# The second norm's turned rows in DRAM: one row of 512 behind the other in the order of the partitions, instead of 32 groups of 8

## The chip, the cores and the metric

The kernel runs on one core of a Trainium2 chip. The time is the device time of one execution in microseconds (us): before the change the median of three runs is 1620.35 us (1619.17 to 1622.79). The core has five engines that run side by side, each with its own instruction stream in order: TensorE (PE) for matmuls, VectorE (DVE), ScalarE (ACT), GpSimd (POOL) and SyncE (SP), which issues nearly all DMAs here. A DMA moves data between DRAM and the core's own memory (SBUF) on up to 16 DMA engines. Matmul results land in banks of a second small memory, PSUM, each of 128 partitions x 512 fp32.

## The reference

One transformer block with adaptive layer norm, in fp32: x has 2048 rows of D = 512.

```python
mod = (_silu(c) @ w_mod).reshape(c.shape[0], 6, 1, -1)
sa, ca, ga, sb, cb, gb = (mod[:, 0], ..., mod[:, 5])
h = _layernorm(x) * (1 + ca) + sa
x = x + ga * _A_ref(h, A_wq, A_wk, A_wv, A_wo)     # 32 heads of 16, one shared key and value head
h = _layernorm(x) * (1 + cb) + sb                  # the second norm
x = x + gb * _B_ref(h, B_w1, B_w2)                 # relu(h @ w1) @ w2, Dff = 1792
return x
```

`_A_ref` is attention of all 2048 rows over all 2048 keys, softmax(q k / 4) v for each head, then a product with wo. The change concerns how h of the second norm gets from the row layout, where the norm is computed, into the turned layout, where `h @ w1` needs it.

## The kernel before, in words

Attention is walked in 32 units: 8 blocks of TB = 256 query rows times NG = 4 groups of heads. For each unit and each of the 16 key tiles (KT) of 128 keys, `scores` (L856) makes four score tiles of 128x512 in PSUM, ACT takes their exponentials into `pe` (L858), and `values` (L999) multiplies these with the values: on PE one step for one key tile, 512 steps in all. One unit ahead, `max_of` (L514, reduced by DVE at L516) computes the maxima that the exponentials subtract.

Between these steps PE does other work in portions (L162 to L178, and L153 to L158 at start and end): for block b the output projection, the first dense layer and the second one. All of this "behind" work of block b runs in the 64 steps of the next block's attention; `behind(b)` (L599) yields it portion by portion. Steps of the other engines that belong to it are put at places in the stream by `at(slot, ...)` (L625): a slot is one step of a key tile, and slot n of block b comes at about step (b + 1) * 64 + n, counted from 0. The order of all instructions is written out by hand, so an engine that reaches an instruction whose data isn't there holds up what is queued behind it.

The second norm of block b (seven blocks; the eighth goes another way in `behind_last` at the end, through PE) takes these steps:

- slots 12 to 20: statistics of the two tiles of 128 rows on DVE, the normed rows `xn` (128 partitions = rows, 512 columns) on POOL, with scale and shift;
- slots 21 and 23, `turn_of(t)` (L647): DVE turns blocks of 32x32 inside `xn` into `xt` (L649), and SyncE writes `xt` to a DRAM tile `xdr` (L651). After the 32x32 turn, partition 32 i + a of `xt` holds, for column number a of every 32-column block, the rows 32 i to 32 i + 31;
- slot 24, `load_turned` (L659): four reads (L663) fetch `xh` from `xdr`, each into 32 partitions, so that a partition holds four columns of h (one of every 128) and along each the 256 rows. They wait for both writes;
- slot 27: two calls of `split` (L255): ACT rounds `xh` to the high part `hh` (L256), and POOL subtracts to get the low part `hl` (L257), since products in the fast fp32 form are made of such parts;
- `dense1` (L575) then multiplies `hh` and `hl` with the first layer's weights; its matmuls show at L175.

In SyncE's queue the order around it is: first write of `xdr`, two loads of the next queries (`qp<-qdr`, L445), second write, the four reads, then the maxima of the next unit (`mdr<-ms`, L478, and `qp<-mdr`, L484). `xdr` has two buffers, so a block writes into another one than the block before; `xh` takes the buffer of `xn`. In block 0 the portions of other work in front of the dense layer are empty (`fill`, L613), so PE has less to do per step there.

Of the kernel before, what the change touches and what calls it, by code (L numbers as in the profile page):

```python
# [9 lines left out]
F32 = mybir.dt.float32  # L10
# [8 lines left out]
S, D, H, DH, DFF = 2048, 512, 32, 16, 1792  # L19
P = 128  # L20
# [4 lines left out]
TT = TB // P  # L25
# [37 lines left out]
def build(tc, nc, cst, sb, ps, dr, x, wq, wk, wv, wo, w1, w2, c, w_mod, out):  # L63
# [11 lines left out]
    def ps_fill():  # L75
        return ps.tile([P, 512], F32, name="ps_fill", tag="fill", bufs=1)
# [149 lines left out]
    def ln_mv(n):  # L226
        return sb.tile([P, n, 2], F32, name="mv", tag="mv", bufs=4)
# [8 lines left out]
    def rsqrt(ve, n, late):  # L236
        y = sb.tile([P, n], F32, name="y", tag="y", bufs=2)
        u = sb.tile([P, n], F32, name="u", tag="u", bufs=2)
        yi = y.bitcast(I32)
        nc.vector.tensor_scalar(yi, ve.bitcast(I32), 1, None, op0=OP.logical_shift_right)  # L240
        nc.vector.tensor_scalar(yi, yi, -1.0, float(0x5f3759df), op0=OP.mult, op1=OP.add)
        for _ in range(3):
            if late:
                nc.vector.tensor_tensor(u, y, y, op=OP.mult)
                nc.vector.scalar_tensor_tensor(u, u, -0.5, ve, op0=OP.mult, op1=OP.mult)
                nc.vector.scalar_tensor_tensor(y, u, 1.5, y, op0=OP.add, op1=OP.mult)
            else:
                nc.gpsimd.tensor_tensor(u, y, y, op=OP.mult)
                nc.gpsimd.tensor_tensor(u, u, ve, op=OP.mult)
                nc.gpsimd.tensor_scalar(u, u, -0.5, 1.5, op0=OP.mult, op1=OP.add)  # L250
                nc.gpsimd.tensor_tensor(y, y, u, op=OP.mult)
        return y
# [25 lines left out]
    def add_psum(dst, pt, other):  # L278
        stg = stage()[:, 0:pt.shape[-1]]
        nc.scalar.activation(stg, pt, AF.Copy)  # L280
        nc.gpsimd.tensor_tensor(dst, stg, other, op=OP.add)
# [267 lines left out]
    def flat(t, k2):  # L549
        return t[:, k2 * 2:k2 * 2 + 2].rearrange("p a n -> p (a n)")  # L550

    def open_block(b):
        x1 = sb.tile([P, TT, D], F32, name="x1", tag="x1", bufs=2)
        nc.sync.dma_start(x1, chunks(x[b * TB:(b + 1) * TB]))
        x1s[b] = x1
        return x1, [sb.tile([P, DC, TB], F32R, name=n, tag="t4", bufs=2) for n in ("oh", "ol")]
# [11 lines left out]
    def normed(x1, xn, ts, nm, y, eng):  # L568
        for n, t in enumerate(ts):
            eng.tensor_scalar(xn[:, t], x1[:, t], nm[:, n:n + 1], y[:, n:n + 1],  # L570
                              op0=OP.add, op1=OP.mult)
            eng.tensor_tensor(xn[:, t], xn[:, t], cbr, op=OP.mult)
            eng.tensor_tensor(xn[:, t], xn[:, t], sbr, op=OP.add)
# [6 lines left out]
    def dense2(b, t, pt):  # L580
        ts = slice(t * P, (t + 1) * P)
        todo = []
        for f in range(FC):
            i, fi = divmod(f, 8)
            rh, rl = r4s[b][i * 2], r4s[b][i * 2 + 1]
            w = w2r[f // 2]
            for n, (a, p) in enumerate(((rh, 0), (rh, 1), (rl, 0))):
                todo.append(("f32r", pt, a[:, fi, ts], w[:, p, f % 2],
                             f + n == 0, f == FC - 1 and n == 2))
        return todo  # L590
# [8 lines left out]
    def behind(b):  # L599
        def in_parts(todo, n):  # L600
            for i in range(0, len(todo), n):
                yield todo[i:i + n]

        def second(b, t):
            pt = ps_fill()
            yield from in_parts(dense2(b, t, pt), 6)
            ot = sb.tile([P, D], F32, name="ot", tag="tmp", bufs=2)
            add_psum(ot, pt, x1s[b][:, t])
            nc.sync.dma_start(out[b * TB + t * P:b * TB + (t + 1) * P], ot)

        x1, oo = open_block(b)
        if b == 0:
            rest, fill = iter([[]] * 3), [[]] * 7  # L613
        else:
            rest, fill = carried.pop(), second(b - 1, 1)
        yield next(rest)
        yield next(rest)
        for k2 in range(DC // 2):
            put_off.append(partial(split, flat(oo[0], k2), flat(oo[1], k2), flat(on[b], k2)))
        yield from rest  # L620
        xn = sb.tile([P, TT, D], F32, name="xn", tag="xn", bufs=1)
        xdr = dr.tile([32, TT, 4, D], F32, name="xdr", tag="xdr", bufs=2)
        mvs = [ln_mv(1) for t in range(TT)]

        def at(slot, *steps):  # L625
            slots.setdefault((b + 1) * 64 + slot, []).extend(steps)

        def norm_of(t, *where):
            st = sb.tile([P, 2, nc.vector.BN_STATS_DIM], F32, name="st2", tag="st2", bufs=2)
            mv = mvs[t]  # L630
            ve = sb.tile([P, 1], F32, name="ve", tag="ve", bufs=2)
            nm = sb.tile([P, 1], F32, name="nm", tag="nm", bufs=2)

            def ends():
                nc.vector.bn_aggr(mv[:, 0], st)
                nc.vector.tensor_scalar(ve, mv[:, :, 1], EPS, None, op0=OP.add)
                nc.gpsimd.tensor_scalar(nm, mv[:, :, 0], -1.0, None, op0=OP.mult)

            def rows():
                normed(x1, xn, (t,), nm, rsqrt(ve, 1, False), nc.gpsimd)  # L640

            for n in range(2):
                at(where[n], partial(nc.vector.bn_stats, st[:, n], x1[:, t, n * TB:(n + 1) * TB]))
            at(where[2], ends)
            at(where[3], rows)

        def turn_of(t):  # L647
            xt = sb.tile([P, D], F32, name="xt", tag="tmp", bufs=2)
            nc.vector.transpose(xt.rearrange("p (j k n) -> p k j n", j=4, k=DC),  # L649
                                xn[:, t].rearrange("p (k j n) -> p k j n", j=4, k=DC))  # L650
            nc.sync.dma_start(xdr[:, t].rearrange("a i n -> i a n"), xt)  # L651

        hp = []
        norm_of(0, *(12, 13, 14, 16))
        norm_of(1, *(17, 18, 19, 20))
        at(21, partial(turn_of, 0))
        at(23, partial(turn_of, 1))

        def load_turned():  # L659
            xh = sb.tile([P, TT * 4, DC, 32], F32, name="xh", tag="xn", bufs=1)  # L660
            pieces = xdr.rearrange("a t i (j m) -> j a (t i) m", j=4)
            for j in range(4):
                nc.sync.dma_start(xh[j * 32:(j + 1) * 32].rearrange("p q k n -> p q (k n)"),  # L663
                                  pieces[j])
            for k2 in range(DC // 2):
                ks = slice(k2 * 2, k2 * 2 + 2)
                at(27, partial(split, *[h[:, ks].rearrange("p k (q n) -> p k q n", n=32)
                                        for h in hp],
                               xh.rearrange("p q k n -> p k q n")[:, ks]))

        at(24, load_turned)
        for t in range(TT):
            pt = ps_fill()
            yield from in_parts(out_proj(pt, oo, t), 6)
            if t == 0:
                add_psum(x1[:, t], pt, x1[:, t])
            else:
                add_psum(x1[:, t, 0:TB], pt[:, 0:TB], x1[:, t, 0:TB])
                nc.vector.tensor_tensor(x1[:, t, TB:], pt[:, TB:], x1[:, t, TB:], op=OP.add)
        ahead = [load_w1(f) for f in range(2)]  # L680

        hp += [sb.tile([P, DC, TB], F32R, name=n, tag="t4", bufs=2) for n in ("hh", "hl")]
        yield from fill
        r4 = r4s[b] = [sb.tile([P, 8, TB], F32R, name="r4", tag="big", bufs=4) for _ in range(4)]
        for f2 in range(FC // 2):
            pt = ps_fill()
            for f in range(f2 * 2, f2 * 2 + 2):
                if f + 2 < FC:
                    ahead.append(load_w1(f + 2))
                yield dense1(pt[:, (f % 2) * TB:(f % 2 + 1) * TB], ahead.pop(0), hp)  # L690
            i, f = divmod(f2 * 2, 8)
            put_off.append(split_psum(
                r4[i * 2][:, f:f + 2].rearrange("p a n -> p (a n)"),
                r4[i * 2 + 1][:, f:f + 2].rearrange("p a n -> p (a n)"), pt, AF.Relu))
        first_half = second(b, 0)
        yield from itertools.islice(first_half, 4)
        carried.append(first_half)
# [225 lines left out]
    for j in range(8):  # L923
# [14 lines left out]
                 t=itertools.chain(*trs), k=itertools.chain(*kvs),  # L938
# [3 lines left out]
    for what in FIRST:  # L942
# [23 lines left out]
        elif what == "s":  # L966
            n = next(sums3)
# [39 lines left out]
    for c in range(NU * KT // 2):  # L1007
# [7 lines left out]
        else:  # L1015
            if not portion:
                banks.extend([ps_max, ps_max, ps_max, ps_fill] * 2)
            u, i, j = places.pop(0)
# [83 lines left out]
```

## Time and profile before

One execution was profiled. Its own time is 1621.31 us, its span (first to last instruction) 1619.5 us.

| what | before |
| --- | --- |
| median of three runs | 1620.35 us (1619.17 to 1622.79) |
| profiled execution | 1621.31 us |
| its span | 1619.5 us |
| PE / DVE / ACT / POOL busy | 1601.0 / 1351.0 / 1210.8 / 383.9 us |
| mean granted clock of PE | 0.999 |
| DMA moved | 137.16 MB in 96198 packets |
| `xdr<-xt` | 14 DMAs of 256 KB, issued from 338.8 to 1445.4 us |
| `xh<-xdr` | 28 DMAs of 128 KB, issued from 350.6 to 1453.8 us |

How to read it: in the profile, `L651` is line 651 of the kernel, `xdr<-xt` names what is written and what is read, `x14` is a count. PE's busy time is the union of matmuls that overlap, and their ends are modelled, so a share near 99% doesn't mean that nothing is late: lateness shows as longer steps between the groups of L999. "Idle before" is the time an engine stood still ahead of an instruction, with the one that ended it. The chain that ended last is followed back from the last instruction to whatever released each step. PEclk is the granted share of PE's clock. In the view by stretches, each row has the stretch, its length, the busy time of PE, PEld (weight loads), DVE, ACT and POOL with the count of instructions, then the granted clock, the mean busy share of the 16 DMA engines, and GB/s. Where the text says a step, it is the time from the start of one group of eight L999 instructions to the next.

### The profile page before, as it was taken

The numbers are of one execution on the slowest core, as the hardware profiler recorded it, in microseconds if no ns is written. First come the engines' busy times: TensorE is split into PE (matmuls) and PEld (weight loads), VectorE is DVE, ScalarE is ACT, GpSimd is POOL, SyncE is SP. The second block draws the span as 40 slices with busy tenths as digits, with TensorE's granted clock in tenths as the row PEclk, the third lists the DMA queues.
The fourth block names the chain that finished last, engine by engine and source line by source line (L and its number), as shares of the span: only waits on it lengthen the run. The fifth ranks groups of instructions, "written<-read, shape, count | busy, mean of one in ns | idle before, by whom it ended". The sixth has DMA issues, their size and how long they took to land.

```text
span 1619.5 us, 33365 instructions
## 1 busy us (share of the span) xinstructions
PE 1601.0 (99%) x12817; PEld 896.0 (55%) x12817; DVE 1351.0 (83%) x2366; ACT 1210.8 (75%) x2372; POOL 383.9 (24%) x584
## 2 busy tenths in 40 slices
PE   9999999999999999999999999999999999999999
PEld 6555554436655565546655565546645565546468
DVE  6888889998889888998889888998889888898031
ACT  4467778778877787778877787778877788778831
POOL 4323455531113110141112211131112211131110
PEclk9999999999999999999999999999999999999999
DMA  8335543213211331214201331113201331113331
GB/s 281 105 114 155 177 115 97 87 55 108 70 36 40 96 105 30 61 43 126 70 22 48 98 105 32 56 48 115 82 20 50 88 105 41 46 59 105 118 121 59
DMA packets 96198, 137.16 MB, mean 85 GB/s; under 512 B 24040, under 2 KB 59564, under 8 KB 96040
## 3 DMA queue, kind: packets, MB, share of 16 engines
q1 hardware_dynamic: 95768, 134.83, 27.6%
q8 instruction: 102, 1.67, 0.4%
q14 instruction: 56, 0.46, 0.1%
q10 hardware_dynamic: 272, 0.20, 0.0%
HBM read 104.00 MB, written 28.82 MB: 82 GB/s over the span
## 4 chain that ended last, share of the span: by engine, by line
PE 91%; DMA 3%; DVE 3%; ACT 1%; issue 1%; SPq 0%; POOL 0%; POOLq 0%; ACTq 0%; DVEq 0%
PE ps_pv L999 30%; PE ps_exp L856 21%; PE ps_fill L175 17%; PE ps_max L514 16%; DVE pm L516 2%; PE ps_fill L158 2%; PE ps_exp L158 1%; DMA xdr<-xt 1%; PE ps_max L158 1%; DMA qdr<-qq 1%; ACT pe L858 1%; PE ps_exp L358 1%; PE ps_exp L149 1%; DMA xh<-xdr 1%; SPq L663 0%
## 5 line engine op out<-in xcount | busy, mean ns | idle before, releaser
L516 DVE TENSOR_REDUCE pm<-ps_max 128x1 f32<-128x512 f32 x2002 | 1247.5, 682 | 152.6 <-PE ps_max L514 108.3
L858 ACT ACTIVATE pe<-ps_exp 128x512 f32<-128x512 f32 x2010 | 1061.9, 604 | 294.4 <-PE ps_fill L175 125.2
L514 PE MATMUL ps_max<-kp,qp 48*128 48x512 f32 x2002 | 822.9, 423 | 1.4 <-DMA qp<-qdr 0.9
L856 PE MATMUL ps_exp<-qp,kp 50*128 50x512 f32 x2010 | 750.2, 415 | 6.9 <-ACT pe L858 6.5
L999 PE MATMUL ps_pv<-pe,vt 128*32 128x512 f32 x4096 | 546.9, 605 | 0.0
L856 PEld LDWEIGHTS ps_exp<-qp,kp 50*128 50x128 f32 x2010 | 352.2, 185 | 296.1 <-ACT pe L858 190.6
L514 PEld LDWEIGHTS ps_max<-kp,qp 48*128 48x128 f32 x2002 | 364.4, 185 | 239.6 <-DVE pm L516 206.3
L175 PE MATMUL ps_fill<-w2r,r 64*128 64x512 f32 x1008 | 274.7, 404 | 0.0
L175 PE MATMUL ps_fill<-hh,w1s 64*128 64x256 f32 x1456 | 211.4, 285 | 0.0
L175 PEld LDWEIGHTS ps_fill<-hh,w1s 64*128 64x128 f32 x1456 | 191.1, 186 | 0.1
L175 PEld LDWEIGHTS ps_fill<-w2r,r 64*128 64x128 f32 x1008 | 174.7, 185 | 7.3
L999 PEld LDWEIGHTS ps_pv<-pe,vt 128*32 128x32 f32 x4096 | 81.3, 108 | 127.5 <-issue 108.4
L257 POOL TENSOR_TENSOR r<-stg,r 128x512 fp32r<-128x512 f32 x49 | 62.8, 1283 | 293.1 <-ACT r L256 286.1
L175 PE MATMUL ps_fill<-hl,w1s 64*128 64x256 f32 x728 | 117.1, 281 | 0.0
L175 PEld LDWEIGHTS ps_fill<-hl,w1s 64*128 64x128 f32 x728 | 97.4, 185 | 0.0
L175 PE MATMUL ps_fill<-hT,wq 64*128 64x256 f32 x320 | 90.6, 399 | 0.0
L1062 POOL TENSOR_TENSOR on<-num,den 128x256 f32<-128x256 f32 x31 | 22.8, 737 | 221.6 <-DMA den<-recs 142.7
L175 PEld LDWEIGHTS ps_fill<-hT,wq 64*128 64x128 f32 x320 | 54.0, 185 | 2.3
L873 POOL COPY num<-pvs 128x256 f32<-128x256 f32 x32 | 12.8, 399 | 162.7 <-ACT pvs L869 151.8
L475 POOL TENSOR_TENSOR ms<-sq,ms 128x32 fp32r<-128x32 f32 x28 | 7.2, 256 | 141.2 <-ACT ms L470 141.2
L268 ACT ACTIVATE stg<-ps_fill 128x512 f32<-128x512 f32 x64 | 39.4, 615 | 0.3 <-PE ps_fill L158 0.2
L175 PE MATMUL ps_fill<-wol,oh 64*128 64x512 f32 x112 | 36.8, 408 | 0.0
(177 smaller groups left out, 1025.0 us busy)
## 6 DMA issues: line engine op xcount, KB each, us to landing
w1s<-w1dr SPq DMA_DIRECT2D x104, 512.0 KB
qp<-qdr SPq DMA_DIRECT2D x64, 192.0 KB
qdr<-qq SPq DMA_DIRECT2D x45, 256.0 KB
raw<-in_B_w_dram SPq DMA_DIRECT2D x28, 256.0 KB
w1dr<-w1s SPq DMA_DIRECT2D x14, 512.0 KB
wmod<-in_w_mod_dram SPq DMA_DIRECT2D x6, 1024.0 KB
x<-in_A_x_dram SPq DMA_DIRECT2D x8, 512.0 KB
out_dram<-ot SPq DMA_DIRECT2D x16, 256.0 KB
```

The source lines that it names most:

```text
L149: nc.tensor.matmul(pt[:, 0:P], idn, idn, start=True, stop=True)
L158: nc.tensor.matmul(pt, w, a, start=start, stop=stop)
L175: ins = nc.tensor.matmul(pt, w[r], a[r], start=start and h == 1, stop=stop and h == 0)
L257: (eng or nc.gpsimd).tensor_tensor(lo, src, hi.bitcast(F32), op=OP.subtract)
L268: nc.scalar.activation(stg, pt, func, **kw)
L358: nc.tensor.matmul(pt, wkv[:, k * P:(k + 1) * P], hT[b][:, k], start=k == 0, stop=k == DC - 1)
L514: nc.tensor.matmul(pt, qps[u][i][r, j * P:(j + 1) * P], kp[r, kb * 512:(kb + 1) * 512], start=True, stop=True)
L516: nc.vector.tensor_reduce(pms[u][:, (hf * 2 + i) * 4 + j, kb:kb + 1], pt, axis=AX.X, op=OP.max)
L856: nc.tensor.matmul(pt, kp[r, kt * P:(kt + 1) * P], qps[u][ct // 2][r], start=True, stop=True)
L858: nc.scalar.activation(pe, pt, AF.Exp)
L999: nc.tensor.matmul(pvt[at:at + 32], vt[:, kt], pes.pop((s, i)), start=(kt == 0), stop=(kt == KT - 1))
L1062: due[1]()
```

## The change

The DRAM tile `xdr` between the write and the reads gets another order of dimensions. Before, it was [32, TT, 4, 512]: for each a of 32, for each tile t, for each i of 4, a row of 512 numbers. Partition p = 32 i + a of `xt` went to row (a, t, i). After, it is [TT, 128, 512]: for each tile t the 128 partitions in their order. The sizes, the number of DMAs and who issues them stay; the pattern by which the write walks DRAM, and that of the reads, change.

```diff
-        xdr = dr.tile([32, TT, 4, D], F32, name="xdr", tag="xdr", bufs=2)
+        xdr = dr.tile([TT, P, D], F32, name="xdr", tag="xdr", bufs=2)
...
-            nc.sync.dma_start(xdr[:, t].rearrange("a i n -> i a n"), xt)
+            nc.sync.dma_start(xdr[t], xt)
...
-            pieces = xdr.rearrange("a t i (j m) -> j a (t i) m", j=4)
+            pieces = xdr.rearrange("t (i a) (j m) -> j a (t i) m", a=32, j=4)
```

On the SBUF side nothing changes: `xt` is written from 128 partitions of 512 numbers each, and each of the four reads fills 32 partitions of `xh` with eight pieces (t, i) of 128 numbers. In DRAM the eight pieces of a partition lay 2 KB apart and the partitions 16 KB apart; now the eight pieces lie 64 KB apart and the partitions 2 KB apart.

## The prediction

> **What bounds the kernel.** I read the page first, for the engine with the least idle time and the chain that ended last.
>
> ```profile
> span 1619.5 us, 33365 instructions
> PE 1601.0 (99%) x12817; PEld 896.0 (55%) x12817; DVE 1351.0 (83%) x2366; ACT 1210.8 (75%) x2372; POOL 383.9 (24%) x584
> PE 91%; DMA 3%; DVE 3%; ACT 1%; issue 1%; SPq 0%; POOL 0%; POOLq 0%; ACTq 0%; DVEq 0%
> PE ps_pv L999 30%; PE ps_exp L856 21%; PE ps_fill L175 17%; PE ps_max L514 16%; DVE pm L516 2%; PE ps_fill L158 2%; PE ps_exp L158 1%; DMA xdr<-xt 1%; PE ps_max L158 1%; DMA qdr<-qq 1%; ACT pe L858 1%; PE ps_exp L358 1%; PE ps_exp L149 1%; DMA xh<-xdr 1%; SPq L663 0%
> ```
>
> TensorE carries 91% of the chain, so only what makes TensorE late can move the end. Yet the two transfers that the change touches, `xdr<-xt` and `xh<-xdr`, stand on that chain. The views of who waited for whom (SyncE's queue, ACT, PE; columns: total us, times, longest) say how much they hold up.
>
> ```profile
> SPq L663 <- DMA xdr<-xt: 41.3, 7, 6.0
> ACT hh L256 <- DMA xh<-xdr: 3.7, 6, 1.8
> ACT hh L256 <- issue: 0.4, 1, 0.4
> PE ps_exp L856 <- ACT pe L858: 6.5, 22, 2.0
> PE ps_exp L746 <- ACT oh L726: 1.4, 2, 1.2
> PE ps_exp L149 <- POOL idn masks.py:199: 1.3, 1, 1.3
> ```
>
> SyncE waits about 6 us in each of 7 blocks for the write, before it can issue the reads. That wait becomes idle time only where ACT comes to `hh` before the rows are back: 3.7 + 0.4 = 4.1 us over seven blocks (the "issue" row is the same instruction in the block whose releaser wasn't told). The longest, 1.8 us, is block 0's. Its chain, and its ACT and PE in order of time:
>
> ```profile
> 343.58 0.61 DVE xt L649
> 344.22 6.32 DMA xdr<-xt
> 350.61 0.61 SPq L663
> 351.27 0.61 SPq L663
> 351.92 0.60 SPq L663
> 352.57 2.98 DMA xh<-xdr
> 358.81 1.53 PE ps_pv L999 x8
> 363.20 0.99 PE ps_pv L999 x8
> 366.06 0.99 PE ps_pv L999 x8
> ```
>
> ```profile
> 353.25 0.59 ACT L858 ACTIVATE pe<-ps_exp 128x512 f32<-128x512 f32 x1
> 355.65 1.15 ACT L256 ACTIVATE hh<-xh 128x512 fp32r<-128x512 f32 x2 [1.82 <-DMA xh<-xdr]
> ```
>
> ```profile
> 354.87 0.50 PE L856 MATMUL ps_exp<-qp,kp 50*128 50x512 f32 x1
> 357.34 0.50 PE L856 MATMUL ps_exp<-qp,kp 50*128 50x512 f32 x1 [1.96 <-ACT pe L858]
> ```
>
> The second write takes 6.32 us to land, four reads go out 0.65 us apart, the last lands 2.98 us later at 355.55, and ACT, free since 353.84, starts `hh` at 355.65. The exponentials behind `hh` on ACT wait too, and TensorE stands 1.96 us for their banks. In a later block (block 1) ACT's row and the chain's L999 rows show the same on a smaller scale:
>
> ```profile
> 540.40 1.15 ACT L256 ACTIVATE hh<-xh 128x512 fp32r<-128x512 f32 x2 [0.31 <-DMA xh<-xdr]
> ```
>
> ```profile
> 537.43 1.00 PE ps_pv L999 x8
> 540.27 1.00 PE ps_pv L999 x8
> 543.55 0.99 PE ps_pv L999 x8
> 546.40 0.99 PE ps_pv L999 x8
> ```
>
> The steps from one key tile to the next are 2.84, 3.28 and 2.85 us: 0.43 too many where ACT idled 0.31, so about 0.12 belongs to `hh` itself, and no later step gives it back. That is the reason to let an idle microsecond of ACT here count as a microsecond of the end.
>
> **The change, part by part.** *The write (L651), 14 times, same 256 KB.* Before, its DRAM side is walked as 4 groups (`i`) of 32 rows (`a`), after as 128 rows in one run. How many of the 16 DMA engines such a write keeps busy can be read from three writes of 256 KB whose outermost counts are 4 (`xdr`, block 6), 8 (`qdr`, dims 8, 16, 512) and 128 (`out`, rows of a contiguous 128x512). In these rows of the view by stretches the last two columns are the share of the 16 engines and GB/s:
>
> ```profile
> 1446.00:1449.00 3.00, 3.00 (x26) 1.40 (x22) 3.00 (x6) 1.99 (x5) 0.00 (x0) 1.00 0.24 53
> 252.20:253.20 1.00, 1.00 (x13) 0.37 (x10) 1.00 (x3) 1.00 (x3) 1.00 (x2) 1.00 0.48 147
> 1608.00:1608.40 0.40, 0.40 (x3) 0.33 (x2) 0.00 (x0) 0.00 (x0) 0.00 (x0) 1.00 1.00 379
> ```
>
> 0.24, 0.48, 1.00: 4, 8 and 16 engines. The new write has the form of `out`'s: xt is [128, 512] on the chip, and xdr[t] is 128 rows of 2 KB behind one another. What that one costs shows at the end of the span, issue and then wait:
>
> ```profile
> 1616.58 0.34 SPq L595 DMA_DIRECT2D out_dram<-ot  x1
> ```
>
> ```profile
> SPq L1098 <- DMA out_dram<-ot: 1.4, 1, 1.4
> ```
>
> 0.34 + 1.4 = 1.74 us is the least from issue to landing; a few short instructions of SyncE lie between, and I take 2.0 as my estimate. The bounds are 1.74 and the present 6.32. So the write lands 6.32 - 2.0 = 4.3 us earlier. SyncE's share of the issue falls too (0.34 against 0.55 to 0.61): at most 14 x 0.25 us on a queue that is idle around it, counted as nothing.
>
> *The first write of each pair* lands early as well. It isn't last: the reads need both, and DVE's second transpose comes 5 us behind the first. It shares the engines with the qp loads issued right behind it, which lands these no later. Nothing gained. Were that cover gone (the second write early), the 2.0 us would be paid there.
>
> *The reads (L663), 28 times, 128 KB each, same 512-byte pieces.* The piece of one partition was 8 runs 2 KB apart, with partitions 16 KB apart; now it is 8 runs 64 KB apart, with partitions 2 KB apart. Counts and outermost size (32 partitions) stay, so the descriptors do. The trace has no such read; the nearest is `qp<-qdr`, whose runs of 1 KB lie 96 KB apart:
>
> ```profile
> 24.60 3.66 DMA qp<-qdr
> ```
>
> At worst by that row 3.66 instead of 2.98 us, at best somewhat under 2.98. I take 2.98, since four reads in flight are paced by their issues (0.65 us each). The last read then lands at 355.55 - 4.3 = 351.25, where ACT wants it at 353.84: 2.6 us of cover in block 0, about 4 in the others. Even the slow bound leaves 1.9.
>
> *What is late next.* With the rows there, `hh` starts when ACT reaches it: block 0 wins 1.82 us, and the PE gap shrinks from 1.96 to about 0.15. The other six win 4.1 - 1.8 = 2.3 us together. Behind the reads SyncE's next issue is the row maxima's:
>
> ```profile
> 353.71 1.71 SPq L478 DMA_DIRECT2D mdr<-ms  x4
> ```
>
> ```profile
> 353.43 0.26 POOL L475 TENSOR_TENSOR ms<-sq,ms 128x32 fp32r<-128x32 f32 x1 [10.64 <-ACT ms L470]
> ```
>
> It starts 0.03 us after POOL's `ms`, not after the reads, so a freer queue brings it nothing. POOL's `hl` follows `hh` and moves with it.
>
> *The clock.* Right behind block 0's stall TensorE's granted clock (the number before the DMA share) halves:
>
> ```profile
> 357.40:359.10 1.70, 1.70 (x10) 0.65 (x14) 1.19 (x2) 1.70 (x5) 1.46 (x2) 1.00 0.38 104
> 359.10:362.60 3.50, 3.50 (x24) 2.23 (x18) 2.03 (x4) 1.92 (x5) 0.00 (x0) 0.51 0.26 103
> 362.60:366.00 3.40, 3.40 (x38) 2.17 (x35) 2.68 (x6) 2.09 (x5) 0.00 (x0) 1.00 0.00 0
> ```
>
> At most 3.5 x 0.49 = 1.7 us are lost; by the L999 rows (358.81 to 363.20 is 4.39 against 2.86 for the next) it is 1.5. The gaps of 1.2 and 1.3 us in the waits above lead to no such drop in the page's clock row; the 1.96 us is the longest of all, so I take the drop as its consequence and as gone: bounds 0 and 1.7, taken 1.5. The Trainium skill (TensorE: Matmul & The Clock Gate, The HAM clock gate) says otherwise in part: a full idle window of about 3.4 us is needed before the clock halves. By that rule a gap of 1.96 us would not cause the drop, and its 1.5 us would stay in the sum; the length of the drop here, 3.5 us, does agree with the page's window.
>
> *Sum:* 1.8 + 2.3 + 1.5 = 5.6 us. The profiled execution took 1621.31 us (span 1619.5 and 1.8 around it), so 1615.7. That execution lies 0.96 above the median of the three runs (1620.35); from the median the same sum gives 1614.75. I forecast 1615.3, between the two.
>
> **The rivals.**
> 1. *The clock drops all the same.* For it: the gap of 1.96 us is not twice as long as those of 1.2 and 1.3 that had no drop behind them, so that something else at this place may bring it, as the first matmuls of the first dense layer, which begin there. Against it: the drop begins 1.8 us after the longest gap of all, and those matmuls run on at 1.00 in all later blocks. Gain 1.8 + 2.3 = 4.1: 1617.2 from the profiled execution, 1616.2 from the median; 1616.9.
> 2. *The new write keeps to few engines, or it is quicker and something else holds `hh`.* Against it are `out`'s row, of the same shape, and that ACT's idle time ends on these rows alone. Then no change, 1620.4.
> 3. *Slower: the reads suffer from the 64 KB distance.* All eight runs of a partition now lie a power of two apart. They decide from the point where the last one, issued 4.3 us earlier, lands later than now: 2.98 + 4.3 = 7.3 us, or 2.4 times as long. At three times (8.9 us) each block loses 1.6, seven lose 11: 1632. Against it: 3.66 us at 96 KB, and the same bytes in as many pieces. The Trainium skill (DMA: Bandwidth & Descriptors, Latency and other measured facts) reports copies slowed by row pitches that are large powers of two, from 207 to 103 GB/s between 512 KiB and 4 MiB; that is twofold, for pitches above this one, and no run here shows it yet. Reads of twice 2.98 us, issued 4.3 us earlier than now, would still be in time in six blocks and 0.4 us late for ACT in block 0: 1615.7.
>
> **How the numbers follow.** Chances: forecast 0.66, rival 1 0.2, rival 2 0.08, rival 3 0.06. The low end takes the best of everything: 1.8 + 2.3 + 1.7, the 0.12 us of `hh` itself in six blocks, and the profile's offset: 1620.35 - 6.5 = 1613.8, rounded down to 1613.3 for the spread of the runs. The high end keeps only the six blocks' 2.3 us: 1621.31 - 2.3 = 1619.0. This holds the forecast and rival 1, and leaves out rivals 2 and 3. A measurement of this kernel can tell about 0.2% (3.2 us) from no change, so faster means under 1617.1. Rival 1 lies about on that line: of its 0.2, half counts as faster and half as the same, and of the forecast 0.63 of 0.66. Faster 0.73, same 0.03 + 0.1 + 0.08 = 0.21, slower 0.06.
>
> **What would show it.** In the changed kernel's profile: a share near 1.0 of the DMA engines during the `xdr` writes, for under 1 us; SyncE's wait at L663 falling from 41.3 us to about 7 x 1.7 = 12; `xh<-xdr` near 3 us to landing; no wait of ACT's `hh` for a DMA; the step of 3.28 us in block 1 at about 2.97; PE's gap of 1.96 us near 0.2, and no clock under 1.00 around 360 us. Wrong would be the prediction if `xh` took 6 us or more, if the gaps of ACT vanish and the L999 steps don't shorten, or if the clock falls elsewhere.

## The result and the profile after

The median of six runs after is 1614.74 us (1614.49 to 1616.42), of six runs before 1620.48 us (1619.11 to 1624.73): ratio 0.9963, 95% interval 0.995 to 0.9976. The change makes the kernel faster by some 5.7 us. The profiled execution took 1614.49 us, 1612.7 of them span.

The page of the changed kernel, its rows for the span, the engines and the chain that ended last:

```profile
span 1612.7 us, 33365 instructions
PE 1596.8 (99%) x12817; PEld 895.3 (56%) x12817; DVE 1350.3 (84%) x2366; ACT 1209.9 (75%) x2372; POOL 384.0 (24%) x584
PE 93%; ACT 2%; DVE 2%; DMA 1%; issue 1%; POOL 0%; SPq 0%; POOLq 0%; ACTq 0%; DVEq 0%
PE ps_pv L999 31%; PE ps_exp L856 21%; PE ps_fill L175 18%; PE ps_max L514 17%; PE ps_fill L158 2%; PE ps_exp L158 1%; PE ps_max L158 1%; DVE pm L516 1%; ACT pe L858 1%; DMA qdr<-qq 1%; DMA wmod<-in_w_mod_dram 1%; PE ps_exp L358 1%; PE ps_exp L325 0%; ACT hT L333 0%; DMA w1t<-w1dr 0%
```

Both transfers are off the chain, DMA's share of it fell from 3% to 1%, and the engines' counts of instructions are what they were. The waits of the changed kernel (total us, times, longest):

```profile
SPq L663 <- DMA xdr<-xt: 11.8, 7, 1.7
PE ps_exp L856 <- ACT pe L858: 4.4, 20, 0.3
```

SyncE waits 1.7 us for a write instead of 6, ACT's `hh` has no row for a DMA any more, and TensorE's longest wait for ACT fell from 2.0 to 0.3 us. While a write moves, about 14 of the 16 DMA engines are busy instead of four (view by stretches, block 6; the share is the column before the last, 0.86):

```profile
1439.70:1440.50 0.80, 0.80 (x10) 0.57 (x8) 0.80 (x2) 0.00 (x0) 0.00 (x0) 1.00 0.86 328
```

The chain's L999 rows around block 0 and around block 1, and ACT's rows at block 1's `hh`, in order of time:

```profile
353.28 1.16 PE ps_pv L999 x8
356.38 0.99 PE ps_pv L999 x8
359.23 0.99 PE ps_pv L999 x8
...
533.44 1.00 PE ps_pv L999 x8
536.29 0.99 PE ps_pv L999 x8
539.16 0.99 PE ps_pv L999 x8
```

```profile
535.52 0.59 ACT L858 ACTIVATE pe<-ps_exp 128x512 f32<-128x512 f32 x1
536.00 1.15 ACT L256 ACTIVATE hh<-xh 128x512 fp32r<-128x512 f32 x2
```

Block 0's two long steps are 3.10 and 2.85 us where they were 5.03 and 4.38 (the ones that ended and began at 358.8), and no gap of PE over 0.15 us stands between them; block 1's long step is 2.87 where it was 3.28. The seven blocks together: 3.46 us in block 0 and 2.90 in the six others (steps of 3.28, 3.26, 3.44, 3.55, 3.36, 3.21 became 2.86 to 2.87), 6.4 in all. The span of these two executions differs by 6.8; the remaining 0.4 lies ahead of the first L999 step, which starts at 93.1 instead of 93.6, where the change does nothing. The clock stays at 1.00 around 360 us:

```profile
358.00:362.00 4.00, 4.00 (x45) 2.79 (x41) 3.67 (x7) 2.98 (x7) 0.00 (x0) 1.00 0.31 121
```

One row was not expected. How long SyncE takes to issue each transfer (ns: least, median, most), first of the kernel before, then after:

```profile
L663 SPq DMA_DIRECT2D xh<-xdr x28: 580/604/699, 350.6 to 1453.8; - x28
L651 SPq DMA_DIRECT2D xdr<-xt x14: 553/572/608, 338.8 to 1445.4; - x14
```

```profile
L663 SPq DMA_DIRECT2D xh<-xdr x28: 302/448/1226, 345.8 to 1442.3; - x28
L651 SPq DMA_DIRECT2D xdr<-xt x14: 314/330/338, 338.3 to 1438.9; - x14
```

The four reads are issued quicker too, typically one of 0.30 and three of 0.45 instead of four of 0.60 us, so the last one leaves 0.6 us sooner behind the first (the 1226 is one read of block 0, which still was back in time). So the change has two halves, and the experiments take them apart.

### The profile page after: what moved, and what is told of

Read it like the earlier page. It is cut to its first block, busy times and chain, and to the rows that moved or that the text cites. A ratio compares the mean times of both kernels' runs of the same rounds, so it can differ in the third digit from the quotient of the medians.

```text
span 1612.7 us, 33365 instructions
## 1 busy us (share of the span) xinstructions
PE 1596.8 (99%) x12817; PEld 895.3 (56%) x12817; DVE 1350.3 (84%) x2366; ACT 1209.9 (75%) x2372; POOL 384.0 (24%) x584
## 4 chain that ended last, share of the span: by engine, by line
PE 93%; ACT 2%; DVE 2%; DMA 1%; issue 1%; POOL 0%; SPq 0%; POOLq 0%; ACTq 0%; DVEq 0%
PE ps_pv L999 31%; PE ps_exp L856 21%; PE ps_fill L175 18%; PE ps_max L514 17%; PE ps_fill L158 2%; PE ps_exp L158 1%; PE ps_max L158 1%; DVE pm L516 1%; ACT pe L858 1%; DMA qdr<-qq 1%; DMA wmod<-in_w_mod_dram 1%; PE ps_exp L358 1%; PE ps_exp L325 0%; ACT hT L333 0%; DMA w1t<-w1dr 0%
## 5 line engine op out<-in xcount | busy, mean ns | idle before, releaser
L999 PE MATMUL ps_pv<-pe,vt 128*32 128x512 f32 x4096 | 546.3, 605 | 0.0
L999 PEld LDWEIGHTS ps_pv<-pe,vt 128*32 128x32 f32 x4096 | 81.3, 108 | 127.4 <-issue 108.2
```

The costliest lines, as they stand in the source:

```text
L999: nc.tensor.matmul(pvt[at:at + 32], vt[:, kt], pes.pop((s, i)), start=(kt == 0), stop=(kt == KT - 1))
```

## The experiments

Ratios are against the kernel before on the same chip; its median was 1622.6 us beside the fast write alone, the new walk alone and the two kernels that take the blocks apart, and 1621.74 beside the other four, so ratios rather than times are compared.

**The fast write alone.** The layout and the reads of before; each write cut into four of 32 partitions.

```diff
-            nc.sync.dma_start(xdr[:, t].rearrange("a i n -> i a n"), xt)
+            for i in range(4):
+                nc.sync.dma_start(xdr[:, t, i], xt[i * 32:(i + 1) * 32])
```

> The layout and the reads of before, but each write is cut into four DMAs of 32 partitions (one for each i), so that the outermost count of each is 32 and not 4. Write theory (the gain comes from 16 instead of 4 DMA engines on the write): the four issues cost some 4 x 0.33 us on SyncE, the last lands about 3.1 us after the first is issued instead of 6.3, the reads go out 3 us earlier, ACT's hh waits for nothing, no clock drop at 360 us: 1614.5 to 1616 us. Reads theory (the gain comes from the reads' new walk, with issues 0.45 instead of 0.60 us): as before the change, 1620.5 us.

1615.9 us, ratio 0.9959 (0.9945 to 0.9973). Its issue times, in the view of one tile's instructions:

```profile
L652 SPq DMA_DIRECT2D xdr<-xt x56: 302/421/543, 338.5 to 1441.5; - x56
L664 SPq DMA_DIRECT2D xh<-xdr x28: 558/602/1285, 348.7 to 1445.3; - x28
```

ACT's row at block 0's `hh`, in order of time:

```profile
353.71 1.15 ACT L256 ACTIVATE hh<-xh 128x512 fp32r<-128x512 f32 x2 [0.26 <-issue]
```

The reads are as slow to issue as before, and `hh` waits only in block 0, for 0.26 us. The write's half gives all that the change gives, within the interval.

**The reads' new walk alone.** The new order, but with an unused row behind each 32, which makes the write 4 groups again.

```diff
-        xdr = dr.tile([TT, P, D], F32, name="xdr", tag="xdr", bufs=2)
+        xdr = dr.tile([TT, 4, 33, D], F32, name="xdr", tag="xdr", bufs=2)
...
-            nc.sync.dma_start(xdr[t], xt)
+            nc.sync.dma_start(xdr[t, :, 0:32], xt)
...
-            pieces = xdr.rearrange("t (i a) (j m) -> j a (t i) m", a=32, j=4)
+            pieces = xdr[:, :, 0:32].rearrange("t i a (j m) -> j a (t i) m", j=4)
```

> The new order of rows, but with a gap of one unused row behind each group of 32 (tile of 2 x 4 x 33 rows), so that the write is again 4 groups of 32 rows, while the reads keep the new walk (runs 66 KB apart). Write theory alone: the write lands after 6.3 to 6.5 us on a quarter of the DMA engines, and the time goes back to 1620.5 us. If the reads' quicker issue counts as well (0.30 + 3 x 0.45 instead of 4 x 0.60 us, 0.6 us in all), ACT's hh waits 0.6 us less than before in each block: some 1.2 us in block 0 and 0 to 0.1 in the six others, so 1616 to 1617.5 us. Reads theory: stays at 1614.7 us.

1617.41 us, ratio 0.9969 (0.9959 to 0.998). The waits of this kernel, then the reads' issue times:

```profile
SPq L663 <- DMA xdr<-xt: 40.7, 7, 6.1
ACT hh L256 <- DMA xh<-xdr: 1.2, 1, 1.2
ACT hh L256 <- issue: 0.3, 1, 0.3
PE ps_exp L856 <- ACT pe L858: 5.8, 22, 1.3
```

```profile
L663 SPq DMA_DIRECT2D xh<-xdr x28: 302/449/841, 350.7 to 1449.3; - x28
```

The write is as slow as ever (6.1 us), yet `hh` waits in two blocks only: 1.2 us in block 0, and 0.25 in block 5, where one read took 0.84 us to issue. The 0.6 us of the reads' issue are enough for waits of 0.2 to 0.6 us. So the six blocks' gain can be had from either half; for the most part the write's is needed in block 0 alone.

**Distance, or form?** The layout of before with an unused row behind each group of 8.

```diff
-        xdr = dr.tile([32, TT, 4, D], F32, name="xdr", tag="xdr", bufs=2)
+        xdr = dr.tile([32, TT * 4 + 1, D], F32, name="xdr", tag="xdr", bufs=2)
...
-            nc.sync.dma_start(xdr[:, t].rearrange("a i n -> i a n"), xt)
+            nc.sync.dma_start(xdr[:, t * 4:t * 4 + 4].rearrange("a i n -> i a n"), xt)
...
-            pieces = xdr.rearrange("a t i (j m) -> j a (t i) m", j=4)
+            pieces = xdr[:, 0:TT * 4].rearrange("a q (j m) -> j a q m", j=4)
```

> The layout of before with an unused row behind each group of 8, so the write is 4 groups of 32 rows as before and the reads' runs are still 2 KB apart, but the partitions lie 18 KB apart and no longer eight run distances, so that the rows of a read can't be taken as one even series of 256. If the reads' quicker issue comes from that (256 rows in one series before, 32 x 8 after): issues of 0.45 us, ACT's waits as in the kernel with the gap of a row behind 32, about 0.9969 of before. If it comes from the distances in DRAM: issues of 0.60 us and the time of before.

1618.1 us, ratio 0.9979 (0.997 to 0.9989). The reads' issue times and ACT's wait:

```profile
L663 SPq DMA_DIRECT2D xh<-xdr x28: 303/448/464, 350.6 to 1448.5; - x28
```

```profile
ACT hh L256 <- DMA xh<-xdr: 1.1, 1, 1.1
```

The runs of a partition still lie 2 KB apart, and the issue takes 0.45 us. So the distance of the runs is not what made it quicker; that of the partitions changed from 16 to 18 KB, which is what breaks the series, and the two can't be told apart here. What the fast cases share is that the 256 rows are no longer one even series; that this is why the issue is quicker fits all four forms run here, but how SyncE's cost arises is not seen.

The time lies above the 0.9969 that was expected from the issue times. The profile doesn't explain it: the profiled execution is the fastest of the nine, 1616.3 us, with a granted clock of 1.000, while seven of the nine lie at 0.998 or 0.999. The clock may have fallen in those; where, no profile shows.

**Block 0 alone, and the other six alone.** The changed kernel, with the layout of before where `grouped` holds (`b == 0` in one kernel, `b > 0` in the other).

```diff
-        xdr = dr.tile([TT, P, D], F32, name="xdr", tag="xdr", bufs=2)
+        grouped = b == 0
+        xdr = dr.tile([32, TT, 4, D] if grouped else [TT, P, D], F32,
+                      name="xdr", tag="xdg" if grouped else "xdr", bufs=2)
...
-            nc.sync.dma_start(xdr[t], xt)
+            nc.sync.dma_start(xdr[:, t].rearrange("a i n -> i a n") if grouped else xdr[t], xt)
...
-            pieces = xdr.rearrange("t (i a) (j m) -> j a (t i) m", a=32, j=4)
+            if grouped:
+                pieces = xdr.rearrange("a t i (j m) -> j a (t i) m", j=4)
+            else:
+                pieces = xdr.rearrange("t (i a) (j m) -> j a (t i) m", a=32, j=4)
```

> The changed kernel with the layout of before in block 0 alone. Write theory with the clock drop as a consequence of the stall: PE's gap of 1.9 us and the half clock at 360 us come back, the steps of L999 there take 5.0 and 4.4 us instead of 3.1 and 2.85, +3.4 us: 1618.2 us. If the clock drop is something else's: +1.9 us without the drop, 1616.6 us.

> The changed kernel with the layout of before in blocks 1 to 6 and the new one in block 0. Write theory: ACT's hh waits 0.2 to 0.6 us in each of the six, each L999 step there is 0.36 to 0.70 us longer, +2.9 us and no clock drop: 1617.6 us. If the six small waits are given back by later steps: 1614.7 us.

Old in block 0: 1618.96 us, ratio 0.9978 (0.9969 to 0.9987). Old in the six: 1618.42 us, ratio 0.9974 (0.9964 to 0.9984). Against the changed kernel's 0.9959 (below) that is 0.19% or 3.1 us for block 0 and 0.15% or 2.4 us for the six; the sizes agree with 3.46 and 2.90, but the intervals are too wide for more. The kernel with block 0 put back, ACT's wait and then three stretches:

```profile
ACT hh L256 <- DMA xh<-xdr: 1.9, 1, 1.9
```

```profile
357.00:359.20 2.20, 0.19 (x2) 0.19 (x2) 0.69 (x1) 1.88 (x4) 1.17 (x1) 1.00 0.06 9
359.20:362.70 3.50, 3.50 (x16) 0.91 (x14) 1.97 (x3) 2.21 (x5) 1.32 (x2) 0.51 0.46 153
92.90:96.50 3.60, 3.60 (x15) 1.20 (x17) 1.66 (x4) 0.00 (x0) 0.00 (x0) 0.53 0.62 179
```

The stall is back and the half clock with it. This execution also has a half clock at 93 us, long before anything that was edited, behind a gap of PE of 0.5 us; so a drop can come without this stall too. In the other kernel ACT's `hh` waits 3.3 us over its six blocks (before: 2.3), 1.1 of them in block 5, where a read took 1.4 us to issue, and the clock is never down before the last 0.4 us of the span.

**The consumer moved, the transfers as before.** The kernel before with the split one slot later:

```diff
-                at(27, partial(split, *[h[:, ks].rearrange("p k (q n) -> p k q n", n=32)
+                at(28, partial(split, *[h[:, ks].rearrange("p k (q n) -> p k q n", n=32)
```

> The kernel before, with the slow write and the slow reads as they were, and only ACT's and POOL's split of xh moved from slot 27 to 28, so that ACT comes to hh 2.85 us later. Wait theory (the end feels the transfers only through ACT's wait at hh): no wait in the six blocks, block 0 loses its 1.8 us too, no half clock at 360 us, so the time of the changed kernel, 0.996 of before, within 1 us. If the transfers themselves hurt (the DMA engines' load): as before. If the dense layer now waits for hh or hl, which come 2.85 us later: up to 2 us a block slower than the changed kernel.

1614.34 us, ratio 0.9958 (0.9945 to 0.997). Its waits:

```profile
SPq L663 <- DMA xdr<-xt: 41.0, 7, 6.0
PE ps_exp L856 <- ACT pe L858: 4.6, 21, 0.3
```

The write takes its 6 us as before, and the whole gain is there. In the profiled execution each of blocks 1 to 6 takes the time that it takes in the changed kernel, to 0.05 us. So, as far as these intervals tell, the end feels the transfers through ACT's wait at `hh` alone, and the dense layer had the time to wait for `hh` a slot longer.

**The consumer moved the other way**, to slot 26:

```diff
-                at(27, partial(split, *[h[:, ks].rearrange("p k (q n) -> p k q n", n=32)
+                at(26, partial(split, *[h[:, ks].rearrange("p k (q n) -> p k q n", n=32)
```

> The kernel before with the split one slot earlier, at 26: ACT comes to hh 2.7 us earlier and waits that much longer in each of seven blocks. Wait theory: 7 x 2.7 = +19 us, 1641 us, if the clock stays up; if each gap of PE over about 2 us halves the clock for 3.4 us, another 1.5 us for each of the six blocks that had no drop, 1650 us. If only a full idle window of 3.4 us halves it, no drops in the six blocks.

1669.01 us, ratio 1.0292 (1.0278 to 1.0306): 47 us slower, more than either figure expected. Waits, then three stretches: the last 1.72 us before the clock falls in block 1, and the half clock of block 1 and of block 6:

```profile
ACT hh L256 <- DMA xh<-xdr: 36.6, 7, 5.7
PE ps_exp L856 <- ACT pe L858: 38.4, 27, 5.3
```

```profile
541.31:543.03 1.72, 0.00 (x0) 0.00 (x0) 1.56 (x4) 0.00 (x0) 0.00 (x0) 1.00 0.64 188
543.03:549.86 6.83, 3.90 (x15) 1.60 (x17) 0.45 (x1) 3.59 (x7) 2.49 (x2) 0.50 0.03 10
1498.76:1505.59 6.83, 6.83 (x31) 2.79 (x31) 2.77 (x4) 3.79 (x8) 1.74 (x3) 0.50 0.02 2
```

The waits grew by 36.6 - 4.1 = 32.5 us instead of the 19 expected, so this slot was 32.5 / 7 = 4.6 us long on ACT and not 2.7. The other 15 us go with the clock, which is down for 6.8 us in each of the seven blocks. PE worked 3.8 (block 0) to 6.8 us (block 6) of each at half speed, 38.2 us in all, which loses at most half of that, 19. (A drop of 3.4 us at about 93 us costs about what the kernel before lost by its own in block 0.) That is enough for the 15 us; how much of it reached the end was not taken apart. So a wait of ACT at `hh` is paid at the end, and a long one is paid a second time in clock.

**The changed kernel once more:**

> The changed kernel once more, to stand beside the three others on the same chip. Both theories: 0.996 of the time of before, steps of 2.86 to 2.87 us in blocks 1 to 6.

1614.57 us, ratio 0.9959 (0.9945 to 0.9973), like the slot moved to 28 and like the fast write alone. No kernel tried is faster than the changed one beyond the intervals; once `hh` doesn't wait, none of these runs shows anything left here to win.

## Why the prediction was right

*The write* (6.32 to an estimated 2.0 us, 16 engines): confirmed. SyncE's wait at L663 is 11.8 us where 12 was expected.

*The reads stay as they are*: wrong, on the good side. The prediction took the issues as 0.65 us apart and held that the descriptors stay; the issues fell to 0.45 (the packets did stay: 96198 in all both before and in the kernel with a gap behind 32), and that half alone removes most of the six blocks' waits. The total didn't suffer, because the two halves overlap: with the write early, the quicker reads find no wait left to remove. The chosen cover (2.6 us in block 0, about 4 in the others) was right or more. The 64 KB distance costs nothing that shows: rival 3 falls. In the kernel whose runs lie 66 KB apart, the last read of block 0 took about as long as the 2.98 us of before:

```profile
352.08 2.90 DMA xh<-xdr
```

The Trainium skill (DMA: Bandwidth & Descriptors, Latency and other measured facts) gives rates for row pitches from 512 KiB (207 GB/s) to 8 MiB (103 GB/s); no run here reaches such pitches, and at 64 KB the trace shows no loss.

*Block 0's stall, 1.8 us, and its clock, 1.5*: 3.3 predicted, 3.46 by the steps. Rival 1 (the clock drops all the same) falls in the two profiles of the changed kernel, and the run with block 0 put back shows the drop come back with the stall. The mean granted clock on record for every execution says more than the profiles: a half clock of 3.4 us takes 1.7 us, or 0.001 of the mean. Of the kernels with block 0's stall of 1.8 us or more, 36 of 44 executions lie under 1.000 (26 of 33 before, 10 of 11 with block 0 put back); of those with no stall there, or one of 0.3 us (the changed kernel, the fast write alone, old in the six, slot 28), 2 of 29 do. So the drop goes with the stall, but not every time: 1.5 us is its size in the one profiled execution, and other executions of the same kernel lost none (1.000) or about twice as much (0.998).

One premise of this step does not hold. The page's clock row prints 9 for every slice of 40 us, the one with the drop too, so it can't show that the gaps of 1.2 and 1.3 us had none. The gap of 1.3 us ends with PE's first instruction, at 1.34 us, while the trace's record of the clock begins at 7.6 us, so it tells nothing. For the gap of 1.2 us, which ends at 1558.98, a stretch behind it does show a full clock in the kernel before:

```profile
1560.60:1564.10 3.50, 3.30 (x15) 2.26 (x13) 2.16 (x3) 0.42 (x1) 0.74 (x1) 1.00 0.96 272
```

*The six blocks, 2.3 us*: mis-sized, 2.90 by the steps. The step that failed is the 0.12 us that the prediction put down to `hh` itself and so kept: block 1's step came out as 2.87, not 2.97. Those 0.12 belong to the wait. ACT's instructions overlap when they follow each other without a gap: the exponential at 535.52 runs 0.59 us, yet `hh` starts 0.48 after it. The exponential in the same place of the kernel before:

```profile
539.50 0.59 ACT L858 ACTIVATE pe<-ps_exp 128x512 f32<-128x512 f32 x1
```

There `hh` started at 540.40, 0.90 after it. A stall thus costs its idle time of 0.31 and the lost overlap of 0.11, 0.42 in all, and the step lost 0.41. The Trainium skill (ScalarE: Activation LUTs, What ACT_TABLE_LOAD costs) gives about 93 ns for this overlap; the trace agrees roughly, with 0.11 us.

*Sum*: 5.6 predicted, 5.7 by the medians (6.4 by the steps of the two profiled executions). From the median the sum gave 1614.75, and 1614.74 was measured. That they meet so closely is luck: the six blocks were 0.6 us short, and the clock's part differs from one execution to the next.

## What to carry to other kernels

Look at the busy share of the DMA engines while one transfer runs alone: here a quarter went with an outermost count of 4, a half with 8, and 0.86 to 1.00 with 128. A layout in DRAM that only the kernel itself reads can be chosen so that the write's outermost count is large. Before making a transfer faster, find the one instruction that waits for it, since its wait, with the overlap and the clock that the gap costs, is all that was won here; moving that instruction one slot later won the same as the faster transfer. A short stall of TensorE can cost more than itself if the clock falls behind it.

## What the runs showed of the hardware that was not expected

- Cutting the even series of 256 rows into 32 x 8 by a gap, or by the order, made SyncE's issue of the same 256 pieces quicker, 0.45 instead of 0.60 us.
- TensorE's clock halved for 3.4 us behind gaps of 1.96 and 2.05 us in block 0 and for 6.8 us behind gaps of 4.6 to 5.3 us. It did not in the one profile with a gap of 1.33 us there and the one with 1.28; but of those two kernels' 16 executions 9 lie under 1.000 in mean clock, so it may have in others. The Trainium skill (TensorE: Matmul & The Clock Gate, The HAM clock gate) asks for a full idle window of about 3.4 us; these runs show drops behind gaps of some 60% of that, and in the slot-26 kernel's block 1 the clock fell when PE had stood still for 1.72 us, so the measurement decides. The lengths, 3.4 and twice 3.4 us, agree with that window. The drop at about 93 us, seen in two kernels' executions (block 0 put back; slot 26) behind gaps of 0.5 us and absent from the others with the same gap, shows that a gap's length isn't the whole condition. One thing that may belong to it: the slot-26 kernel's seven long drops begin 187.7 us and then five times 191.1 us apart, which is 55 and 56 times 3.413 us, although the gaps before them don't lie so evenly. The drops thus begin on a grid of that step, and where a gap lies on it may count too; no run varies that alone, so the condition stays open.
